# A list schedule that gives a token gather a longer way to its landing, and one conditional part at the end instead of two

## The chip, the cores and the metric

The kernel runs on 1 core of one Trainium2 chip. The metric is the device time of one execution in microseconds, as the median of several runs. Engines are named as in the profile: PE is TensorE's matmul, PEld its weight load, DVE is VectorE, ACT ScalarE, POOL GpSimd, SP SyncE. A "q" behind an engine's name marks rows of its sequencer.

## The reference, cut to what matters

Three layers follow each other: chunked attention, a dense layer, and a layer of 8 experts of which each of 3072 tokens uses the one with the largest logit. The change lies in the third.

```python
def _moe2_ref(x, modality_id, w_gate, modality_bias, w1, w2):
    logits = x @ w_gate + modality_bias[modality_id]      # (3072, 8)
    e_idx = np.argmax(logits, axis=1)
    probs = softmax(logits)
    gate_w = probs[np.arange(N), e_idx]
    for e in range(E):
        mask = e_idx == e
        h = np.maximum(x[mask] @ w1[e], 0.0)              # 512 -> 1024
        out[mask] = gate_w[mask, None] * (h @ w2[e])      # 1024 -> 512
```

## The kernel before, in words

**Order of the work.** All work is cut into units, each of one engine, with a length in the plan, a time until others see the result (`extra`), the units that it comes after and the tiles that it touches. `Plan.order` (lines 89 to 156) puts them in order before the program is built: each unit gets a rank, the longest way from it to the end in planned lengths, extras and slacks between units (600 ns where nothing else is given, 120 ns under the name HOP). Then, step by step, the unit is taken whose start, less 0.003 of its rank, is smallest (lines 119 to 134). A start is the latest of the engine's planned idle time, the planned ends of what it comes after, and a free slot for its tiles. What comes out is one order of instructions for each engine; the planned times themselves are not on the chip, where each engine waits for semaphores alone. A unit that waits holds back all that stands behind it on its engine.

**Stages.** Attention goes through 32 sub-blocks, the dense layer through 8 blocks of 384 tokens (`dense`, line 543), each with 16 pairs of products h and y on PE, in three float32r passes. One h of 384 columns is 12 matmuls, one y of three groups of 128 tokens is 9; each is a unit of 1950 ns in the plan. `in_turn` (line 533) fixes their order on PE over all tiles: h, h, y, h, y and so on, so that the first h of a tile stands between the last two y of the tile before. After each block, `routing` (line 569) computes the logits, scales the rows by their gates, stores them in DRAM (`yd`), and enters the tokens in a table of each expert's tokens. The table's entries come out of a small product on PE (`place`, line 677, unit `tm`, tile `tp`) and are added on DVE (`enter`, unit `ta`).

**Experts.** A tile of tokens is up to 384 tokens of one expert (3 groups of 128) or a small one of up to 128. Two tiles, e0 and e1, belong to the expert that is largest after 7 of the 8 blocks and start while the last block is still computed. Then come the lists that `plan_list` (line 797) computes on DVE: `planb`, 15 places for large tiles b0 to b14, and `plans`, 8 places for small ones s0 to s7. Six large tiles and one small one are always computed (`N_BIG`, `N_SMALL`). What is over these counts is computed in two conditional parts at the end of the program (lines 1083 to 1092): each loads a count of tiles from the tile `ei` into a register of each engine, compares, and branches over its instructions if nothing is over. With this input neither part is entered.

**Tokens of a tile** (`tokens`, line 857). DVE computes the tile's indices (`ids`, units `id`, tile `gi`), after the first h of the tile before. For each of the 3 groups POOL issues an indirect DMA that gathers 128 rows from DRAM (`gather`, line 889, unit `ga`, 1040 ns in the plan, tile `xg`); PE transposes them (`turn`, line 894, unit `tx`, tile `xp`, 4 small matmuls in line 896); ACT casts them (`high`, tile `xh`, line 899), DVE subtracts for the low part (`low`, tile `xl`, line 903). The first h of the tile reads both. The gather's time until others see the result is `extra=DMA_LAG + 800`, which is 2700 ns (line 910). The units `tx` have a boost, so that PE takes them as soon as the plan has them ready.

**Weights.** SP loads the expert's weights some units ahead (`weights`, line 926), ACT and DVE split them into high and low parts. Tiles of tokens and of weights share 36 slots of the tag `w`.

The scatter of a tile's results is an indirect DMA of POOL, too (`put`, line 1054).

Of the kernel before, what the change touches and what calls it, by code (L numbers as in the profile page):

```python
# [12 lines left out]
I32 = mybir.dt.int32  # L13
# [26 lines left out]
HOP = 120.0  # L40
DMA_LAG = 1900.0
BOOST = 20000.0
TAIL_BOOST = 40000.0
# [18 lines left out]
class Plan:  # L62
    """Units of work, each of one engine, put in order by a list schedule.

    A unit has an estimated length (and time until others see its result), the units it comes after and the tiles it
    touches; a tile holds a slot of its tag from the first unit that touches it to the end of the last.
    """

# [96 lines left out]
def kernel(  # L165
# [50 lines left out]
    g0 = const.tile([P, E], F32, name="g0")  # L216
    ei = const.tile([P, 3 + MAX_ST + E], I32, name="ei")
    masks = const.tile([QB, 3, P], BF16, name="masks")
# [24 lines left out]
    def U_seq(name, ns, steps, after=(), tiles=(), **kw):  # L243
        """A chain of VectorE units, one for each operation of a generator; name.k is the k-th, name itself the last."""
        gen = []

        def step(last):
            if not gen:
                gen.append(steps())
            next(gen[0], None)  # L250
            if last:
                for _ in gen[0]:
                    pass

        for i, n in enumerate(ns):
            last = i == len(ns) - 1
            U(name if last else f"{name}/{i}", "DVE", n, lambda last=last: step(last), [f"{name}/{i - 1}"] if i else after, tiles, **kw)

# [1 line left out]
    def constants():  # L260
# [40 lines left out]

        # the routing bias of each token, by its modality
        T.new("mi", "w", [P, NTILE, 2], I32)
# [20 lines left out]

# [1 line left out]
    # two heads go through the array at once, with zeros between them (q and k come with head pairs' columns as rows); the  # L326
    # first blocks' scores, for which the other engines have no time, are float32 products, the later three float32r passes
    def attention(n):
# [37 lines left out]
        def parts_of(key, i):  # L366
            """Of q all; of k the i-th half, the second heads' rows, which go into the right columns."""
            x, to = T[f"qk{n}"], T[f"qs{n}" if key == "q" else kb]
            if key == "q":
                return [to[:, 0], to[:, 1]], x[:, :, 0:QB]  # L370
            r = slice(64 * i, 64 * i + 64)
            return [to[r, e, :, P * i:P * i + P] for e in range(2)], x[r, :, QB:]
# [17 lines left out]
        def minima(i):  # L390
            """Of the negated scores."""
            for h in (2 * i, 2 * i + 1):
                dve.tensor_tensor_reduce(  # L393
                    out=T[f"pt{n}"][:, h, :], in0=T[f"sc{n}.{i // 2}"][:, h % 4, :], in1=mask, scale=-scale, scalar=3.0e38,
                    op0=ALU.add, op1=ALU.min, accum_out=T[f"mn{n}"][:, h:h + 1])
# [59 lines left out]

# [1 line left out]
    def conversion(f):  # L457
# [57 lines left out]

# [1 line left out]
    def prod_h(hp, xh, xl, wh, wl, n):  # L517
# [15 lines left out]
    def in_turn(h, y):  # L533
        """Keeps the products of both layers in turn: h, h, y, h, y, ..."""
        if chain:
            T.units[h][3].append(chain[-1][0])
            T.units[chain[-1][1]][3].append(h)
        if len(chain) > 1:
            T.units[h][3].append(chain[-2][1])
            T.units[y][3].append(chain[-1][1])  # L540
        chain.append((h, y))
# [23 lines left out]

# [1 line left out]
    O_t = {}  # L567

    def routing(j):
# [115 lines left out]
        def order(t, e):  # L685
            """Two experts' columns at a time."""
            return [f"lm{j}.{TPB - 1}.{e - 2}"] if e >= 2 else []
# [28 lines left out]

# [1 line left out]
    jobs = {}  # L718
# [37 lines left out]
    def plan_counts():  # L756
# [24 lines left out]
        yield  # L781
        # group of the s-th tile of the list = s + f[its expert]; f is summed up from its steps
        pool.memset(fb[:, E:E + 1], float(NG))
# [13 lines left out]
    def plan_list(nm):  # L797
        end, f, n, at, move = plan[nm]
        s16 = [P, n, E]
        c2, df, ex = parts(T["plan" + nm], n * E, E, n)  # L800
        dve.tensor_tensor(out=df, in0=f[:, 1:E + 1], in1=f[:, 0:E], op=ALU.subtract)
        yield
        c2 = c2.rearrange("p (s e) -> p s e", e=E)
        dve.tensor_tensor(out=c2, in0=bm(end, s16), in1=bc(iota[:, 0:n], s16), op=ALU.is_le)
        yield
        dve.tensor_reduce(out=ex, in_=c2, op=ALU.add, axis=AX.X)
        yield
        dve.tensor_scalar(out=ei[:, at:at + n], in0=ex, scalar1=float(E - 1), scalar2=None, op0=ALU.min)
        yield
        dve.tensor_tensor(out=c2, in0=c2, in1=bm(df, s16), op=ALU.mult)  # L810
        yield
        g = small([P, n], "g" + nm)
        dve.tensor_reduce(out=g, in_=c2, op=ALU.add, axis=AX.X)
        yield
        dve.tensor_scalar(out=g, in0=g, scalar1=f[:, 0:1], scalar2=None, op0=ALU.add)
        yield
        if move:
            dve.tensor_tensor(out=g, in0=g, in1=iota[:, 0:n], op=ALU.add)
            yield
        dve.tensor_scalar(out=g, in0=g, scalar1=float(NG), scalar2=None, op0=ALU.min)  # L820
        yield
        for i in range(n):
            jobs[nm, i].update(g=g[:, i:i + 1])
        last = 1 + MAX_ST + E + (0 if move else 1)
        dve.tensor_copy(out=ei[:, last:last + 1], in_=end[:, E - 1:E])
        yield

    def planning():
# [11 lines left out]
        U_seq("planb", [130] * 10, lambda: plan_list("b"), ["pc"], ["plan", "planb"])  # L840
        U_seq("plans", [100] * 9, lambda: plan_list("s"), ["pc"], ["plan", "plans"])
        ready = [f"st{NBLK - 2}.{t}" for t in seven]
# [14 lines left out]
    def tokens(s, prev):  # L857
        """Which tokens the tile has, their rows of y, and those turned for the products."""
        job, nm = jobs[s], nm_of(s)
# [48 lines left out]
        for t in range(nt):  # L908
            x = f"{nm}.{t}"
            U(f"ga{x}", "Pool", 1040, lambda t=t: gather(t), [f"id{nm}/{gi}"], [f"xg{x}", f"gi{nm}"], extra=DMA_LAG + 800, **F)  # L910
            U(f"tx{x}", "PE", 430, lambda t=t: turn(t), [f"ga{x}"], [f"xg{x}", f"xp{x}"], **F)
            U(f"tH{x}", "ACT", 480, lambda t=t: high(t), [f"tx{x}"], [f"xp{x}", f"xh{nm}"], **F)
            U(f"tL{x}", "DVE", 600, lambda t=t: low(t), [f"tH{x}"], [f"xp{x}", f"xh{nm}", f"xl{nm}"], **F)
# [12 lines left out]
    def weights(s, x, use, used, loads):  # L926
        """One tile of the expert's weights: loads, and the two parts; use is the product that it is for."""
        job = jobs[s]
# [65 lines left out]
    def small_step(s, g, used, y_after):  # L994
        """P tokens stay in the array and half of w1's columns pass by; their products are turned for the second layer."""
        nm = nm_of(s)
# [67 lines left out]

# [1 line left out]
    with tc.manual_schedule():  # L1066
# [15 lines left out]
        at = 1 + MAX_ST + E  # L1082
        for nm, n0, n1, col in (("b", N_BIG, MAX_ST, at), ("s", N_SMALL, E, at + 1)):
            cnt = nc.values_load(  # L1084
                ei[0:1, col:col + 1], min_val=0, max_val=n1,
                skip_runtime_bounds_check_because="a count of tiles that the number of tokens and experts bounds")
            with tc.If(cnt > n0):
                T.restart()
                chain.clear()
                begin.clear()  # L1090
                experts([(nm, i) for i in range(n0, n1)])
                T.emit()

# [29 lines left out]
def laid_out(name, inputs):  # L1123
    """q and k come in blocks, with two heads' columns as rows; v with a row's heads side by side, k and v with the memory rows after the context."""
    a = inputs[name]
# [50 lines left out]
```

## Time and profile before

| | |
|---|---|
| runs, us | 1023.49, 1021.09, 1030.64 (median 1023.49) |
| span of the profiled execution, us | 1021.5 |
| PE busy, us | 959.6 (94%) |
| DVE, ACT, POOL busy, us | 724.1, 479.0, 218.2 |
| mean granted TensorE clock | 0.975 |
| HBM read and written, MB | 97.20, 12.85 |

The profiled execution's own time is not recorded beside its span; of the three runs 1021.09 is 0.4 us under the span and 1023.49 is 2.0 us over it. The span goes from the first instruction to the last. The granted clock is a share of the full 2.4 GHz; its other level is 1.2 GHz.

How to read it: PE is busy nearly all of the span, so the questions are where it is not, and what it waited for there. A wait that the profile puts down to a DMA names the transfer whose landing came last.

### The profile page before, as it was taken

To read this page: it belongs to the slowest core of one execution; us is meant where nothing else is said; L and a number is where in the kernel's file an instruction comes from. 1 tells how busy PE (TensorE), PEld (TensorE's weight loads), DVE (VectorE), ACT (ScalarE), POOL (GpSimd) and SP (SyncE) were. 2 spreads that over 40 slices of the span, in tenths; PEclk is the share of its full clock that TensorE was granted. 3 is DMA by queue.
4 is the path that set the end of the run, shared out by engine and by line. 5 is a ranking of instruction groups with operands and counts; after the bars stand their busy time and mean duration, and the time that the engine had idled before them with its cause. 6 is when DMAs were issued, how large, how long until landed. Compare 5 with 4: busy or idle time off the path is not lost. (4 is left out here: it accounts for less than half of the span.)

```text
span 1021.5 us, 15964 instructions
## 1 busy us (share of the span) xinstructions
PE 959.6 (94%) x5356; PEld 847.6 (83%) x5356; DVE 724.1 (71%) x2031; ACT 479.0 (47%) x1273; POOL 218.2 (21%) x186
## 2 busy tenths in 40 slices
PE   6696899999999999999999999998999999999994
PEld 3575778889889889889889888997998888988983
DVE  5999988957966975984993993775975455544550
ACT  5666665626535544544553452224233344433541
POOL 6678552101201201111120210001012021112101
PEclk8789989999999999999999999999999999999998
DMA  9825421221231230221321211136057455456311
GB/s 285 271 77 169 132 70 50 89 90 50 78 101 30 82 117 20 81 89 42 99 72 59 88 43 42 42 101 218 22 179 232 153 169 176 138 163 208 129 49 44
DMA packets 99458, 110.99 MB, mean 109 GB/s; under 512 B 18623, under 2 KB 73695, under 8 KB 99360
## 3 DMA queue, kind: packets, MB, share of 16 engines
q1 hardware_dynamic: 95360, 96.96, 30.0%
q0 software_dynamic: 4000, 12.85, 3.8%
q8 instruction: 46, 0.75, 0.3%
q14 instruction: 52, 0.43, 0.1%
HBM read 97.20 MB, written 12.85 MB: 108 GB/s over the span
## 5 line engine op out<-in xcount | busy, mean ns | idle before, releaser
L411 POOL TENSOR_TENSOR pt<-pt,rs 96x512 f32<-96x512 f32 x64 | 83.8, 1328 | 411.7 <-DVE rs L406 332.3
L400 ACT ACTIVATE pt<-pt,mn 96x128 f32<-96x128 f32 x256 | 99.5, 392 | 42.6 <-DVE mn L393 42.5
L495 POOL TENSOR_TENSOR wm<-wm,wt 128x512 int32<-128x512 int32 x32 | 49.9, 1568 | 24.7 <-DVE wm L484 16.6
L400 ACT ACTIVATION_READ_ACCUMULATOR pt<-pt,mn 96x1 f32 x256 | 48.5, 190 | 0.0
L380 DVE TENSOR_TENSOR pad<-qk,pad 64x512 fp32r<-64x512 f32 x48 | 45.5, 947 | 0.7
L423 PE MATMUL pv<-px,v 128*64 128x96 f32 x512 | 30.9, 267 | 9.0 <-DVE mn L393 5.6
L423 PEld LDWEIGHTS pv<-px,v 128*64 128x64 f32 x512 | 24.5, 147 | 16.5 <-issue 12.7
L376 ACT CAST pad<-qk 64x512 fp32r<-64x512 f32 x48 | 29.5, 614 | 0.8 <-DMA qk<-in_k_dram 0.3
L502 POOL TENSOR_TENSOR wl<-wm,wh 128x512 fp32r<-128x512 f32 x16 | 24.8, 1548 | 5.2 <-ACT wh L498 5.2
L426 ACT CAST xh<-pv 128x384 fp32r<-128x384 f32 x32 | 15.1, 474 | 17.7 <-PE pv L423 17.7
L498 ACT CAST wh<-wm 128x512 fp32r<-128x512 f32 x32 | 19.6, 618 | 7.0 <-POOL wm L495 7.0
L393 DVE DVE_READ_ACCUMULATOR2_ANT mn<- 96x1 f32 x256 | 20.2, 79 | 0.0
L502 DVE TENSOR_TENSOR wl<-wm,wh 128x512 fp32r<-128x512 f32 x16 | 19.3, 1208 | 0.5 <-ACT wh L498 0.5
L480 DVE TENSOR_SCALAR wm<-wm 128x1024 int32<-128x1024 int32 x16 | 17.1, 1069 | 1.3 <-ACT wm L476 1.3
L890 POOL DMA_INDIRECT xge0.0_7148<-yd,gie x1 | 1.2, 1174 | 77.7 <-DMA rawxe0.1_7118<-in_moe_w_dram 77.7
L429 DVE TENSOR_TENSOR xl<-pv,xh 128x384 fp32r<-128x384 f32 x32 | 17.4, 547 | 0.0
L380 DVE TENSOR_TENSOR qs<-qk,qs 128x384 fp32r<-128x384 f32 x24 | 16.4, 682 | 0.5
L592 DVE DVE_READ_ACCUMULATOR2_ANT lg<- 128x1 f32 x192 | 15.7, 82 | 0.0
L376 ACT CAST qs<-qk 128x384 fp32r<-128x384 f32 x24 | 12.3, 512 | 0.2
L405 DVE TENSOR_SCALAR rs<-sm 96x8 f32<-96x8 f32 x32 | 9.6, 299 | 1.2 <-ACT pt L400 1.2
L632 DVE TENSOR_SCALAR ya<-ya,rg 128x512 f32<-128x512 f32 x16 | 7.4, 501 | 0.2
L406 DVE RECIPROCAL rs<-rs 96x8 f32<-96x8 f32 x32 | 6.4, 199 | 1.1
(6397 smaller groups left out, 3218.5 us busy)
## 6 DMA issues: line engine op xcount, KB each, us to landing
v<-in_v_dram SPq DMA_DIRECT2D x32, 256.0 KB, 2.7
qk<-in_k_dram SPq DMA_DIRECT2D x24, 256.0 KB, 3.2
qk<-in_q_dram SPq DMA_DIRECT2D x24, 192.0 KB, 3.3
yd<-ya SPq DMA_DIRECT2D x16, 256.0 KB, 2.1
pad<-in_k_dram SPq DMA_DIRECT2D x16, 128.0 KB, 3.9
yd<-yb SPq DMA_DIRECT2D x8, 256.0 KB, 2.5
qs<-in_q_dram SPq DMA_DIRECT2D x8, 192.0 KB, 4.5
wd0.0_114<-in_moe_w_in_dram SPq DMA_DIRECT2D x1, 512.0 KB
```

Of the source, the lines that this page charges most:

```text
L376: act.copy(out=to[0], in_=x)
L380: dve.tensor_tensor(out=to[1], in0=x, in1=to[0].bitcast(F32), op=ALU.subtract)
L393: dve.tensor_tensor_reduce(out=T[f"pt{n}"][:, h, :], in0=T[f"sc{n}.{i // 2}"][:, h % 4, :], in1=mask, scale=-scale, scalar=3.0e38, op0=ALU ...
L400: act.activation(out=pt[:, h, :], in_=pt[:, h, :], func=AF.Exp, bias=T[f"mn{n}"][:, h:h + 1], scale=-1.0, accum_out=T[f"sm{n}"][:, h:h + 1])
L411: pool.tensor_tensor(out=pt[:, half, :], in0=pt[:, half, :], in1=bc(T[f"rs{n}"][:, half], [QB, 4, P]), op=ALU.mult)
L423: pe.matmul(T[f"pv{n}"][r:r + 64, h // 2, :], T[f"v{n}"][:, D * h:D * h + D], T[f"px{n}"][:, h, :], start=True, stop=True)
L429: dve.tensor_tensor(out=T[f"xl{j}"][:, :, cols], in0=T[f"pv{n}"], in1=T[f"xh{j}"][:, :, cols].bitcast(F32), op=ALU.subtract)
L480: dve.tensor_scalar(out=mi, in0=mi, scalar1=3, scalar2=None, op0=ALU.logical_shift_left)
L495: pool.tensor_tensor(out=mi, in0=mi, in1=T[f"wt{f}"][:, i], op=ALU.add)
L498: (dve.tensor_copy if f in D_CH else act.copy)(out=T[f"wh{f}"][:, i], in_=T[f"wm{f}"][:, i])
L502: e.tensor_tensor(out=T[f"wl{f}"][:, i], in0=T[f"wm{f}"][:, i], in1=T[f"wh{f}"][:, i].bitcast(F32), op=ALU.subtract)
L592: dve.tensor_tensor_reduce(out=part(products), in0=part(y_at[t]), in1=T[f"wg{j}.{e // 2}"][:, e % 2], scale=1.0, scalar=0.0, op0=ALU.mult, ...
```

## The change

`GATHER_LAG = 6500.0` takes the place of `DMA_LAG + 800` (2700) as the planned time from a gather's issue unit to its landing. The scatter keeps `DMA_LAG + 800`. The two conditional parts become one, with the bodies of both. It is entered if a sum of two comparisons is above zero: `planb` writes "more than six large tiles" into the last column of the tile `plan`, and `plans`, which now comes after `planb`, adds "more than one small tile" and writes the sum into one column of `ei`, which is one column shorter. Comments and docstrings are left out of the changed file; line numbers stay but for the one added line.

```diff
 DMA_LAG = 1900.0
+GATHER_LAG = 6500.0
...
-    ei = const.tile([P, 3 + MAX_ST + E], I32, name="ei")
+    ei = const.tile([P, 2 + MAX_ST + E], I32, name="ei")
...
         for i in range(n):
             jobs[nm, i].update(g=g[:, i:i + 1])
-        last = 1 + MAX_ST + E + (0 if move else 1)
-        dve.tensor_copy(out=ei[:, last:last + 1], in_=end[:, E - 1:E])
+        if move:
+            dve.tensor_scalar(out=T["plan"][:, DM - 1:DM], in0=end[:, E - 1:E], scalar1=float(N_BIG), scalar2=None, op0=ALU.is_gt)
+        else:
+            dve.scalar_tensor_tensor(out=ei[:, at + n:at + n + 1], in0=end[:, E - 1:E], scalar=float(N_SMALL), in1=T["plan"][:, DM - 1:DM], op0=ALU.is_gt, op1=ALU.add)
         yield
...
-        U_seq("plans", [100] * 9, lambda: plan_list("s"), ["pc"], ["plan", "plans"])
+        U_seq("plans", [100] * 9, lambda: plan_list("s"), ["pc", "planb"], ["plan", "plans"])
...
-            U(f"ga{x}", "Pool", 1040, lambda t=t: gather(t), [f"id{nm}/{gi}"], [f"xg{x}", f"gi{nm}"], extra=DMA_LAG + 800, **F)
+            U(f"ga{x}", "Pool", 1040, lambda t=t: gather(t), [f"id{nm}/{gi}"], [f"xg{x}", f"gi{nm}"], extra=GATHER_LAG, **F)
...
         at = 1 + MAX_ST + E
-        for nm, n0, n1, col in (("b", N_BIG, MAX_ST, at), ("s", N_SMALL, E, at + 1)):
-            cnt = nc.values_load(
-                ei[0:1, col:col + 1], min_val=0, max_val=n1,
-                skip_runtime_bounds_check_because="a count of tiles that the number of tokens and experts bounds")
-            with tc.If(cnt > n0):
-                T.restart()
-                chain.clear()
-                begin.clear()
-                experts([(nm, i) for i in range(n0, n1)])
-                T.emit()
+        more = nc.values_load(
+            ei[0:1, at:at + 1], min_val=0, max_val=2,
+            skip_runtime_bounds_check_because="a sum of two results of comparisons")
+        with tc.If(more > 0):
+            T.restart()
+            chain.clear()
+            begin.clear()
+            experts([("b", i) for i in range(N_BIG, MAX_ST)] + [("s", i) for i in range(N_SMALL, E)])
+            T.emit()
```

## Rows read from the trace of the kernel before

**Rows 1.** The page, part 1: busy time of the engines, share, instructions.

```profile
PE 959.6 (94%) x5356; PEld 847.6 (83%) x5356; DVE 724.1 (71%) x2031; ACT 479.0 (47%) x1273; POOL 218.2 (21%) x186
```

**Rows 2.** Waits of PE from 640 us on: us in total, times, longest us.

```profile
PE xpb5.2_9557 L896 <- DMA xgb5.2_9510<-yd,gib: 2.0, 1, 2.0
PE xpe0.1_7220 L896 <- DMA xge0.1_7156<-yd,gie: 1.6, 1, 1.6
PE xpe0.0_7212 L896 <- DMA xge0.0_7148<-yd,gie: 1.2, 1, 1.2
PE xpb3.2_8875 L896 <- DMA xgb3.2_8828<-yd,gib: 0.9, 1, 0.9
...
PE xpb1.2_8193 L896 <- DMA xgb1.2_8146<-yd,gib: 0.8, 1, 0.8
PE hpxb0.0_8040 L521 <- ACT xhb L899: 0.7, 1, 0.7
PE xpb2.2_8534 L896 <- DMA xgb2.2_8487<-yd,gib: 0.7, 1, 0.7
PE xpb4.2_9216 L896 <- DMA xgb4.2_9169<-yd,gib: 0.5, 1, 0.5
```

**Rows 3.** Line 1084, register loads: ns min/median/max, first and last start us.

```profile
L1084 POOLq TENSOR_LOAD <-ei x2: 308/407/506, 1008.5 to 1014.5; - x2
```

**Rows 4.** Line 1087, the conditional parts: ns min/median/max, first and last start us.

```profile
L1087 POOLq EVENT_SEMAPHORE  x8: 17/43/3405, 1009.6 to 1015.3; - x8
...
L1087 PEldq COMPARE_BRANCH  x2: 3884/4128/4372, 1004.0 to 1008.5; - x2
...
L1087 POOLq COMPARE_BRANCH  x2: 45/45/45, 1009.1 to 1014.9; - x2
...
L1087 POOLq INC_SWDGE_SEM  x2: 1157/1172/1188, 1013.3 to 1015.4; - x2
```

**Rows 5.** Line 1171, the program's end: ns min/median/max, first and last start us.

```profile
L1171 POOLq DRAIN  x3: 40/107/4148, 1016.6 to 1021.3; - x3
```

**Rows 6.** Timeline of PE at e1's transposes: start us, us, engine, line, operation.

```profile
718.57 0.60 PE L896 MATMUL xpe1.0_7439<-ident,xge1.0_7382 128*128 128x128 f32 x4
...
719.36 0.95 PE L521 MATMUL hpxe0.3_7450<-xhe,ehxe0.3_7205 128*128 128x384 f32 x4
```

**Rows 7.** Timeline of PE at b1's transposes.

```profile
791.12 0.60 PE L896 MATMUL xpb1.0_8182<-ident,xgb1.0_8102 128*128 128x128 f32 x4
...
793.32 0.94 PE L521 MATMUL hpxb0.3_8200<-xhb,ehxb0.3_7921 128*128 128x384 f32 x4
...
795.49 0.39 PE L527 MATMUL ypb0.0_8105<-ehxb0.2_7910,ghxb0.2_8161 128*128 128x512 f32 x1
```

**Rows 8.** Timeline of PE at b5's transposes.

```profile
933.36 0.60 PE L896 MATMUL xpb5.0_9546<-ident,xgb5.0_9466 128*128 128x128 f32 x4
...
936.79 1.53 PE L521 MATMUL hpxb4.3_9564<-xhb,ehxb4.3_9393 128*128 128x384 f32 x4
...
940.52 0.39 PE L527 MATMUL ypb4.0_9469<-ehxb4.2_9358,ghxb4.2_9525 128*128 128x512 f32 x1
```

**Rows 9.** Windows: us, busy of PE, PEld, DVE, ACT, POOL, PEclk, DMA share, GB/s.

```profile
937.00:941.00 4.00, 4.00 (x16) 3.92 (x15) 0.69 (x1) 0.87 (x2) 1.00 (x1) 0.59 1.07 375
```

**Rows 10.** Timeline of PE at e0's and b0's transposes and first products, with tp7.

```profile
699.39 0.60 PE L896 MATMUL xpe0.2_7247<-ident,xge0.2_7181 128*128 128x128 f32 x4
...
706.08 0.86 PE L521 MATMUL hpxe0.0_7302<-xhe,ehxe0.0_7145 128*128 128x384 f32 x4
...
763.95 0.25 PE L679 MATMUL tp7.0_7919<-ab7.0_7689 128*128 128x192 f32 x1
...
774.69 0.60 PE L896 MATMUL xpb0.0_8017<-ident,xgb0.0_7980 128*128 128x128 f32 x4
...
778.43 0.97 PE L521 MATMUL hpxb0.0_8040<-xhb,ehxb0.0_7867 128*128 128x384 f32 x4 [0.68 <-ACT xhb L899]
```

**Rows 11.** Timeline of ACT at b0's transposes.

```profile
775.33 0.59 ACT L899 CAST xhb<-xpb0.0_8017 128x512 fp32r<-128x512 f32 x1 [2.02 <-PE xpb0.0_8017 L896]
```

## The prediction

> **What bounds the kernel now.** I read the page's first part, then PE's waits from 640 us on, then the timeline around each wait, and last the sequencer rows of the end. Nearly the whole span is TensorE's: 959.6 of 1021.5 us [rows 1]. From 640 us on, when the routed experts come into play, the list of PE's waits is short, and all but one of its longest entries have one form: the transposes of gathered tokens (line 896) wait for the gather's DMA, and once a first product waits for the cast behind the transposes [rows 2]. So in this stage a microsecond of PE wait is a microsecond of the run, and weights, activations and the other engines end no wait there. After the last product comes a stretch without PE work, in which Pool's queue sets the end [rows 3 to 5].
>
> **What a wait costs.** Undisturbed, two groups of transposes take 719.36 - 718.57 = 0.79 us, 0.44 for the first and 0.35 for each further one [rows 6], so three take 1.14. At b1 they took from 791.12 to 793.32, 2.20 us [rows 7]: 1.06 lost, of which 0.8 is the wait listed and 0.27 the restart. With the same restart b2, b3 and b4 lost 0.7, 0.9 and 0.5 plus three times 0.27, which is 2.91. e0 had two waits, 1.6 and 1.2 [rows 2], and lost 3.34. At b5 the three took from 933.36 to 936.79, so 2.29 were lost, and the product group behind took 940.52 - 936.79 = 3.73 us [rows 8] where the one after b1's took 2.17 (793.32 to 795.49): 1.56 more. The granted clock was 0.59 in that stretch [rows 9], part of it at the lower of the two levels, 1.2 GHz, after PE had stood still for 2.0 us. I book those 1.56 with the wait before them. b0 lost 778.43 - 774.69 - 1.14 = 2.60 [rows 10].
>
> **Part 1: the lag.** No instruction is added or removed; the schedule gives each engine another order. GATHER_LAG replaces 2700 ns by 6500, so the plan holds transposes ready 3.8 us later. In the plan a PE unit is 1950 ns, so they move back past two units of products; on the chip a unit is 2.17 us at most, so PE reaches them some 4.2 us later, less what it no longer waits.
>
> b1 to b5: these tiles are gathered right after the tile before has begun, and PE has ten units of that tile left when the transposes come (hpxb0.3 follows at 793.32). The latest landing against its place was b5's, 936.40; the third transposes would then stand at 933.36 + 4.2 + 0.79 = 938.3, so 1.9 us to spare. All of it goes: 1.06 + 2.91 + 2.29 + 1.56 = 7.8 us. What is late next is the tile's first product, and that is eight units off after the move.
>
> e0: its third transposes stood at 699.39 and its first product at 706.08, with three units between [rows 10]. Two units later one unit (2.1 us) is left, in which 0.35 of transposes, a cast of 0.59 [rows 11] and a subtraction, which I take as 0.7, must fit: 1.64. It fits by half a microsecond, and the low part is read only by the second third of the products. I take 3.3; the bounds are 0 and 3.34.
>
> b0: here nothing else can stand between, since the order of products is fixed by the code (line 533: h, h, y, h, y) and the first product of b0 comes right after the transposes. What can help is an earlier gather. Its indices wait for the table of the last block, whose small products (line 679) stood at 763.95 [rows 10], long after their inputs. PE picks the ready unit with the longest way to go. By the code's own costs and slacks the way from tp7 to b0's first product is 11,915 planned ns with the old lag; from the y that follows tp7 it is 11,790, from the h ahead of tp7 13,860, and from the y ahead of that 16,410. This is why tp7 stands where it does; with 15,715 it passes one unit, not two. So gather and landing come 2.1 us earlier, transposes run in one go at 774.69, and then ScalarE's three casts of 0.59 set the pace: the first began at 775.33 [rows 11], three in a row end at 777.16, not 778.43. I take 1.2; bounds 0 (no earlier gather) and 2.60.
>
> What moves with it: tp7's additions on DVE go ahead of one or two weight subtractions, and transposes' casts move on ACT and DVE. Neither engine ends a PE wait here except in the b0 case. The gathers themselves keep their places behind the tile's indices in Pool's queue; on SP the plan may shift a weight load by a unit, since token tiles hold their slots 3.8 us longer in the plan. No PE wait in [rows 2] ends on a weight, so I count that as nothing; uncovered it would be a wait like those of the list, 0.5 to 2.0 us.
>
> Part 1 sums to 7.8 + 3.3 + 1.2 = 12.3 us, between 0 and 13.8.
>
> **Part 2: one conditional part.** The two copies of a count (line 825) become two comparisons of one column each, and plans now follows planb. That is DVE time beside PE's products of e1, and no entry of [rows 2] ends on a DVE operation; uncovered it would be a wait like the smallest of the list, 0.5 us. At the end each engine loses one register load, one branch and one set of waits. Only Pool's copy matters: it goes through the first part, waits for the last scatter's landing (3.4 us), raises a semaphore (1.19 us), then goes through the second from its load at 1014.5 to the drain at 1016.6 [rows 3 to 5]. This second pass, 2.1 us, goes. The drain of 4.15 us stays, I assume. The bounds: 0, if the drain waits for something with a time of its own, and 4.2, if it works off two raises of 2.1 us each and has one left. I take 2.1, as the drain's row is one instruction that begins where the pass ends.
>
> On Pool the branch takes 0.05 us; on PE the same branch took 3.9 to 4.4 [rows 4]. The merged body is longer, so Pool's branch could come to cost what PE's does. It would lie beside the landing wait of 3.4 us, so at most 4.4 - 3.4 = 1.0 us of the 2.1 would be given back. The Trainium skill (Runtime: NRT & Kernel Launch, section Instruction fetch mechanics) says that a taken branch to a target outside the instruction window waits for a fetch; by that rule the longer body speaks against this part, with PE's branches agreeing and Pool's not showing it.
>
> **Sum.** 12.3 + 2.1 = 14.4 us: a span of 1007.1 us for the profiled execution's 1021.5. The three runs lie between 1021.09 and 1030.64 with a median of 1023.49; the span is beside the lower two, so I take the difference from the median: 1009.0 us.
>
> **The rivals.** (1) The wait only changes its place at e0 and b0: the first product waits for the cast or subtraction instead. For it: [rows 2] has such a wait at hpxb0.0, 0.7 us, and e0's spare is 0.5 us. Against: e0's casts have PE work beside them. Then 7.8 + 2.1 = 9.9 us are won: 1013.6, inside one per cent. (2) The end gives nothing, by the drain's own time or Pool's branch together: 12.3 won, 1011.2. For it: the drain is longer than anything else there. Against: nothing in flight is seen behind the last scatter's landing. (3) The change doesn't do what it says: transposes come later, but the gathers land later too, because they and the weight loads share the DMA engines, or the plan moves gathers and transposes together. Then only the end is won: 1021.4. Against: a gather is issued as soon as its indices are there, which the lag doesn't touch. (4) Slower: the longer lag puts transposes so late that each tile's first product waits, as at b0, long enough for the clock to fall as at b5. The place is the first h of e0 to b5; seven such tiles at b5's 3.85 us are 27 us, against 13.8 + 2.1 lost now, so 11 us slower: 1034. It decides against the change from 2.3 us per tile on. For it: b5's rows show the price. Against: b1 to b5 have eight units to spare, and only e0 and b0 are close.
>
> **How the numbers follow.** Forecast 0.62, rival 1 0.20, rival 2 0.08, rival 3 0.06, rival 4 0.04. A measurement of this kernel tells about 1 per cent from no change (the three runs alone lie 0.9 per cent apart), so faster by over 1 per cent means under 1013.3 us. Of the forecast 0.60 and of rival 2 0.07 lie there: 0.67. Within 1 per cent are rivals 1 and 3 and 0.03 of the others: 0.29. Slower: 0.04. The range reaches down to all waits gone and a drain halved (18.0 won, 1005.5) and up to rival 1 with another term of 3 us missing (1016.5).
>
> **What would show it.** Right: PE's waits from 640 us on lose every entry on a gather's DMA, transposes of b1 to b5 stand two product units further on, tp7 stands one unit earlier, the clock stays at 1.00 around b5, and Pool has one register load and one raise before its drain. Wrong: a wait of a first product (hpxe0.0, hpxb0.0) on xh or xl above 1.5 us; waits on gathers of the old size in new places; a drain that grew by what the pass lost; new waits on weights.

## The result, and the profile after

The changed kernel takes 1007.39 us (median of four runs, 1006.8 to 1008.51) beside 1023.13 of the kernel before in the same runs: a ratio of 0.984, with a 95% interval from 0.9801 to 0.9878. The profiled execution has a span of 1006.7 us, 14.8 less than the one before; its own time is 1008.51. The prediction was 1009.0 and a span of 1007.1, so the sum came out. Two of its terms did not, and they cancel in part, so some of that closeness is luck. Two of the ten runs of one experiment below, the merge alone, were slow (1342.14 and 1562.1 us, at a granted clock of 0.652 and 0.555) and are left out of its median.

First PE's waits, the same view and nearly the same stretch as [rows 2] (us in total, times, longest):

```profile
PE hpxb0.0_8040 L522 <- ACT xhb L902: 0.7, 1, 0.7
PE xpb0.2_8030 L899 <- DMA xgb0.2_7987<-yd,gib: 0.6, 1, 0.6
PE htxs0.1_10148 L1034 <- ACT hrxs0.1_10141 L1044: 0.2, 1, 0.2
```

That is the whole list from 630 us on (line numbers are up to three higher than before). The waits on gathers of e0 and of b1 to b5 in [rows 2] are gone; one at b0 is left, and b0's wait for the cast is unchanged. Before, b0 had two waits on gathers, one of 0.3 us and this one, which [rows 2] leaves out:

```profile
PE xpb0.1_8022 L896 <- DMA xgb0.1_7987<-yd,gib: 0.9, 1, 0.9
```

At b5 the transposes used to stand in one block and wait [rows 8]. Now, in the timeline of PE:

```profile
927.58 0.60 PE L899 MATMUL xpb5.0_9560<-ident,xgb5.0_9465 128*128 128x128 f32 x4
927.93 0.48 PE L528 MATMUL ypb4.0_9469<-ehxb4.2_9358,ghxb4.2_9528 128*128 128x512 f32 x1
...
930.09 0.60 PE L899 MATMUL xpb5.1_9590<-ident,xgb5.1_9485 128*128 128x128 f32 x4
930.53 0.60 PE L899 MATMUL xpb5.2_9595<-ident,xgb5.2_9495 128*128 128x128 f32 x4
930.88 0.94 PE L522 MATMUL hpxb4.4_9601<-xhb,ehxb4.4_9432 128*128 128x384 f32 x4
```

The first group stands one unit later (behind an h) and the other two groups two units later (behind the y that follows). No row has a wait in brackets. The granted clock in that stretch, transposes and the products behind them, columns as in [rows 9]:

```profile
927.00:935.00 8.00, 8.00 (x47) 7.21 (x46) 4.92 (x9) 4.60 (x9) 1.22 (x2) 1.00 0.42 160
```

1.00, the upper level, stands where 0.59 stood. PE was busy all 8 us ahead of and behind the transposes; the fall of the clock went with the wait.

At e0 the transposes stand two units later, as predicted. One unit, a y of block 7, is left between the third group and the first product:

```profile
697.09 0.60 PE L899 MATMUL xpe0.0_7247<-ident,xge0.0_7150 128*128 128x128 f32 x4
...
700.08 0.60 PE L899 MATMUL xpe0.2_7279<-ident,xge0.2_7182 128*128 128x128 f32 x4
702.60 0.86 PE L522 MATMUL hpxe0.0_7302<-xhe,ehxe0.0_7132 128*128 128x384 f32 x4
```

At b0 the small products tp7.1 and tp7.2 moved up by one unit, ahead of an h (tp7.0 moved further, to 743.92), and two short waits are left (in brackets: idle time, and what ended it):

```profile
758.60 0.25 PE L680 MATMUL tp7.1_7898<-ab7.1_7708 128*128 128x192 f32 x1
...
771.47 0.60 PE L899 MATMUL xpb0.0_8017<-ident,xgb0.0_7966 128*128 128x128 f32 x4
...
773.15 0.66 PE L899 MATMUL xpb0.2_8030<-ident,xgb0.2_7987 128*128 128x128 f32 x4 [0.65 <-DMA xgb0.2_7987<-yd,gib]
774.49 0.97 PE L522 MATMUL hpxb0.0_8040<-xhb,ehxb0.0_7870 128*128 128x384 f32 x4 [0.68 <-ACT xhb L902]
```

The end, to be read beside [rows 3 to 5] (ns minimum/median/maximum, first and last start):

```profile
L1086 POOLq TENSOR_LOAD <-ei x1: 498/498/498, 996.9 to 996.9; - x1
```

```profile
L1089 POOLq EVENT_SEMAPHORE  x4: 17/42/2323, 997.9 to 998.2; - x4
...
L1089 PEldq COMPARE_BRANCH  x1: 3778/3778/3778, 992.5 to 992.5; - x1
...
L1089 POOLq COMPARE_BRANCH  x1: 45/45/45, 997.5 to 997.5; - x1
...
L1089 POOLq INC_SWDGE_SEM  x1: 1188/1188/1188, 1000.5 to 1000.5; - x1
```

```profile
L1173 POOLq DRAIN  x3: 40/107/4148, 1001.8 to 1006.5; - x3
```

One load, one branch, one raise of a semaphore (INC_SWDGE_SEM); the drain has the same 4148 ns; Pool's branch costs 0.045 us as before. But there is one difference that the prediction did not have: the wait for the last scatter's landing is 2.32 us, where it was 3.41.

Where the time went, by stages. The starts of first products are read from the timelines of PE, and the stages are their differences in us:

| stage | before | after | won |
|---|---|---|---|
| start to block 7's first h | 633.93 | 634.10 | -0.17 |
| to e0's first h | 72.15 | 68.50 | 3.65 |
| to e1's first h | 34.74 | 34.94 | -0.20 |
| to b0's first h | 37.62 | 36.95 | 0.67 |
| to b5's first h (b1 to b5's transposes) | 180.74 | 173.06 | 7.68 |
| to PE's last product | 48.51 | 48.60 | -0.09 |
| to the span's end | 13.87 | 10.58 | 3.29 |
| span | 1021.55 | 1006.73 | 14.82 |

### The profile page after: what moved, and what is told of

Same layout as the page of the kernel before. It is cut to its first block, busy times and chain, and to the rows that moved or that the text cites. A ratio compares the mean times of both kernels' runs of the same rounds, so it can differ in the third digit from the quotient of the medians.

```text
span 1006.7 us, 15940 instructions
## 1 busy us (share of the span) xinstructions
PE 958.3 (95%) x5356; PEld 848.1 (84%) x5356; DVE 721.9 (72%) x2031; ACT 477.8 (47%) x1273; POOL 221.7 (22%) x186
## 5 line engine op out<-in xcount | busy, mean ns | idle before, releaser
L496 POOL TENSOR_TENSOR wm<-wm,wt 128x512 int32<-128x512 int32 x32 | 49.9, 1568 | 25.2 <-DVE wm L485 16.4
L893 POOL DMA_INDIRECT xge0.0_7150<-yd,gie x1 | 1.2, 1171 | 77.2 <-DMA rawxe0.1_7102<-in_moe_w_dram 77.2
```

The source lines that it names most:

```text
L496: pool.tensor_tensor(out=mi, in0=mi, in1=T[f"wt{f}"][:, i], op=ALU.add)
```

## The experiments

In what follows "the end" is the time from PE's last product to the span's end, and "from block 7" is the sum of the last six stages of the table (387.62 before, 372.63 after). That sum leaves out the first 634 us, which differ by up to 4.1 us between executions of kernels that are nearly alike there (632.5 to 636.6). It is therefore finer than the medians, but it is read from one execution of each kernel.

**Each part alone.** The lag on the kernel before:

```diff
-            U(f"ga{x}", ..., extra=DMA_LAG + 800, **F)
+            U(f"ga{x}", ..., extra=GATHER_LAG, **F)
```

> The lag alone, with both conditional parts kept as before. Theory (a wait of PE costs its length and a restart of 0.27 us; the second pass at the end costs 2.1 us): PE waits as in the changed kernel, Pool's second pass is back, 1007.4 + 2.1 = 1009.5 us. Rival (all 3.2 us by which the stretch behind the last product is shorter come from the merged part): 1010.6 us, with a last scatter that lands in 4.5 us as before. Rival (the end gives nothing): 1007.4 us.

Measured: 1011.27 us (1010.55 to 1012.49), ratio 0.988 [0.9864, 0.9897]; from block 7 374.97 us; PE's waits are b0's 0.8 and s0's 0.3 alone. The end is 13.85 us, as before. The lag is thus worth 12.7 us of the 15.0 in this view. In this execution b0's transposes waited for no gather, and e1's to b0's first product took 36.19 us, 0.8 less than in the changed kernel. The end speaks for the first rival, that the merge gives all of the 3.2 us there; 2.1 us for it was too little.

The merge alone, which is the changed kernel with the old lag:

```diff
-GATHER_LAG = 6500.0
+GATHER_LAG = 2700.0
```

> The merged part alone, with the old lag of 2700. Theory: all waits on gathers as before, one pass less at the end, 1023.1 - 2.1 = 1021.0 us; if b5's wait is again 2 us, the clock falls behind it again and costs 1.5 us. Rival (the end gives 3.2 us): 1019.9 us. Rival (the fall of the clock at b5 was an accident of one execution): no fall with the same wait.

Measured: 1020.1 us (median of eight runs, 1015.1 to 1023.82), ratio 0.997 [0.9947, 0.9993]; from block 7 383.53; the end is 10.27 us. So the merge gives 3.6 us at the end with the old lag (13.87 less 10.27) and 3.3 with the longer one (13.85 less 10.58), and again 2.1 was too little. PE's waits are those of [rows 2] with other sizes. The windows of this run show the clock again (columns as in [rows 9]; behind e0's waits, behind b0's, behind b5's):

```profile
697.00:700.50 3.50, 3.50 (x15) 3.41 (x14) 0.72 (x2) 0.60 (x2) 0.00 (x0) 0.53 1.05 378
778.50:782.50 4.00, 3.40 (x11) 3.40 (x12) 1.18 (x3) 0.54 (x1) 0.00 (x0) 0.57 0.40 132
935.50:939.50 4.00, 2.81 (x18) 2.80 (x19) 1.82 (x3) 1.05 (x3) 0.16 (x1) 1.00 1.07 383
```

The clock went to the lower level, 1.2 GHz, for most of a stretch at e0 (behind a wait of 2.2 us) and at b0 (behind 1.0, 0.3 and 0.7), and not at b5 (1.4), where it fell in the kernel before. A fall comes behind such waits, but not in a fixed place. The sizes of the waits are those of one execution.

**The size of the lag**, by the same line:

```diff
-GATHER_LAG = 6500.0
+GATHER_LAG = 4600.0
```

> The changed kernel with half the added lag, 4600. The order on PE shows the transposes of b1 to b5 one unit later than before, those of e0 one unit later, and two of three tp7 products where they stood before. Theory (each wait is set against the place of the transposes): waits of b1 to b4 (0.5 to 0.9) gone, b5's 2.0 down to 0.1 or less and no fall of the clock, e0 keeps one wait of 1.0, b0 loses 2.6 as before; 2.5 us over the changed kernel, 1009.9 us. Rival (the gain is from the order at large, not from these places): as the changed kernel, 1007.4 us, or half of the gain gone, 1014 us.

Measured: 1012.03 us, ratio 0.9883 [0.9866, 0.9899]; but from block 7 373.22, only 0.6 over the changed kernel, and PE waits at b0 (0.7 and 0.5) and s0 alone. The expected wait at e0 is not there. The profiled spans lie 3.1 us apart, and 2.5 of these lie in the first 634 to 636.6 us, ahead of all gathers; the changed kernel itself took 634.10 and 636.39 us for them in its two profiles. What is left of the 4.6 us between the medians no profile shows.

And with `GATHER_LAG = 10300.0`:

> The changed kernel with twice the added lag, 10300. The order on PE shows all three transposes of e0 right ahead of its first product, and tp7 two units earlier than in the changed kernel. Theory: nothing more to win at b1 to b5; e0's first product now waits for casts, about 1.3 us lost; b0's gather lands before PE comes to it, so its wait on the DMA (0.65) goes and only the wait for casts stays; 0.7 us over the changed kernel, 1008.1 us. Rival (a longer lag makes each tile's first product wait): over 1015 us.

Measured: 1008.8 us, ratio 0.9855 [0.9839, 0.9872]; from block 7 372.55. Here the transposes of e0 stand right before its first product, and rival 1 of the prediction shows itself at e0 (timeline of PE):

```profile
701.97 0.60 PE L899 MATMUL xpe0.2_7289<-ident,xge0.2_7184 128*128 128x128 f32 x4
703.35 0.96 PE L522 MATMUL hpxe0.0_7302<-xhe,ehxe0.0_7131 128*128 128x384 f32 x4 [0.78 <-ACT xhe L902]
```

It costs 1.2 us at e0 (69.71 against 68.50 us to e0's first h). Most of that is paid back at b0 (36.07 against 36.95), where the gathers come earlier and no wait for a DMA is left. So from 4600 to 10300 the place of the transposes is worth less than 1 us: what counts is that they stand behind the landing at all.

**The end.** Why does one part less give 3.3 to 3.6 us when its pass on Pool lasted 2.1? To tell a second part's own price from what comes with its length, a second part with a tiny body was put behind the merged one:

```diff
+        second = nc.values_load(
+            ei[0:1, at:at + 1], min_val=0, max_val=2,
+            skip_runtime_bounds_check_because="a sum of two results of comparisons")
+        with tc.If(second > 0):
+            nc.vector.tensor_copy(out=ei[:, at:at + 1], in_=ei[:, 0:1])
```

> The changed kernel with a second conditional part behind the one it has: the same flag is loaded again, and its body is a single small DVE copy. What is read is the end: from PE's last product to the span's end it took 13.9 us with two long parts, 10.2 to 10.6 with one; the last scatter took 4.5 to 4.6 us from issue to landing with two, 3.0 to 3.4 with one. Theory: a second part costs Pool a pass of 2.1 us whatever its length, while the scatter's later landing comes from instruction fetches of the second branches that share DMA engines with it, and a branch over a tiny body needs none: tail 12.3 to 12.7 us, scatter 3.0 to 3.4 us, as many instruction packets beside the scatter as in the changed kernel (4). Rival A: a second part delays the scatter by its loads and waits, however short: tail 13.6 to 13.9, scatter 4.5. Rival B: the pass of a tiny part hides in the landing wait: tail 10.2 to 10.6.

Measured: the end is 10.74 us (1009.21 us in all, ratio 0.9864 [0.9829, 0.99]); the scatter takes 3.0 us. So the theory was right on the scatter and wrong on the pass. The tiny part costs Pool a load of 0.30 us and a branch of 0.045, some 0.5 us in all, with no raise:

```profile
L1095 POOLq TENSOR_LOAD <-ei x1: 304/304/304, 999.4 to 999.4; - x1
```

A raise of 1.2 us therefore belongs to the long body, which has DMAs of Pool in it, and not to a conditional part as such; it is over half of the 2.1 us. Whether the DMAs or the length bring it was not tested. What delays the scatter can be seen in the DMA queues. Packets, MB and share of the 16 engines' time during the last scatter, from its issue to the end of its landing wait, first before (4.6 us):

```profile
q0 software_dynamic: 80, 0.20, 14.6%
q14 instruction: 4, 0.03, 2.8%
q8 instruction: 1, 0.02, 2.8%
```

after (3.4 us):

```profile
q0 software_dynamic: 80, 0.20, 16.1%
q14 instruction: 3, 0.02, 2.8%
q8 instruction: 1, 0.02, 1.8%
```

the lag alone, with two parts (4.7 us):

```profile
q0 software_dynamic: 80, 0.20, 17.3%
q8 instruction: 2, 0.03, 4.5%
q14 instruction: 4, 0.03, 2.7%
...
out_dram<-bys0.0_10185,sxs POOLq DMA_INDIRECT x1, 4.6
```

and the merged part with the tiny one behind (3.2 us):

```profile
q0 software_dynamic: 80, 0.20, 16.2%
q14 instruction: 3, 0.02, 3.0%
...
out_dram<-bys0.0_10185,sxs POOLq DMA_INDIRECT x1, 3.0
```

The scatter is always the same 80 packets. Beside them the two kernels with two long parts have one instruction packet more on q14, and their large ones on q8 take 2.8% of 16 times 4.6, which is 2.06 us, and 4.5% of 16 times 4.7, which is 3.4 us for two; after the change the one packet takes 1.8% of 16 times 3.4, 0.98 us. They are read here as what branches fetch: PE's second branch begins at 1008.5 and takes about 4 us [rows 4], so it lies beside the scatter, issued at 1008.74. The Trainium skill (Runtime: NRT & Kernel Launch, section Instruction fetch mechanics) says that an engine fetches its instructions by DMA in blocks of 16 KiB, and that a taken branch out of the window forces such a fetch. The packets of q8 agree (44 for 0.72 MB on the page after, 16.4 KB each), and so do PE's branches, 3.3 us over the long body and 0.24 over the tiny one in the run with both; Pool's branch of 0.045 us, over a body of the same kind, shows no wait for one. Other runs fall in line: without any instruction packet beside it the last scatter landed in 2.6 us (the run without a part, below), without one of q8 in 3.0 to 3.2 (six runs with one long part), beside one short one of q8 in 3.4 (both profiles of the changed kernel), and beside the long ones in 4.6. That the fetches delay the scatter is how these views are read here. No run delayed the scatter by fetches alone.

To see what the remaining part costs, it was left out; large tiles over six and small ones over one are then not computed, and with this input there are none:

```diff
-        more = nc.values_load(
...
-        with tc.If(more > 0):
...
```

> The changed kernel without any conditional part (large tiles over six and small ones over one are then never computed; with this input there are none). Theory: Pool's remaining pass, raise included, goes as the second one went, and the scatter has no branch's instruction fetch beside it: tail 10.4 less 2.1, so 8.0 to 8.5 us, with the drain of 4.15 us still there, and a scatter of 3.0 us or less from issue to landing. Rival A: the raise of 1.2 us belongs to the drain and stays: tail 9.2 to 9.6. Rival B: the drain waits for something with a time of its own: tail unchanged, 10.2 to 10.6, with a longer drain.

Measured: the end is 6.84 us, under every one of the three expectations (1005.02 us in all, ratio 0.9816 [0.9779, 0.9852]). The rows of Pool's last scatter and of its drain:

```profile
997.12 0.98 POOL L1058 DMA_INDIRECT out_dram<-bys0.0_10185,sxs  x1 [3.32 <-ACT bys0.0_10185 L1055]
```

```profile
L1164 POOLq DRAIN  x3: 40/107/5373, 996.9 to 1002.8; - x3
```

The drain begins beside the scatter's issue (its row starts at 996.9 and lasts 5.37) and ends 4.2 us after that issue (996.9 + 5.37 - 998.10), while the scatter lands 2.6 us after its start. So the drain has a time of its own of about 4.15 us behind Pool's last work, and runs beside the landing; a scatter that lands later than that was not tested. What waits for the landing is the skipped part: 2.3 us, and then its raise of 1.2. That is 3.5 of the 3.7 us by which this end is shorter than the changed kernel's 10.58.

If so, that price should go when the part is passed before the last scatter is there. The last scatter was moved behind it (its source tile takes the room of bias and masks):

```diff
             T.emit()
+        late[0]()
```

> The changed kernel with the last scatter (small tile s0) issued behind the conditional part instead of ahead of it; its source tile takes the room of the bias and the masks, which are done with by then. Without any conditional part the end took 6.84 us from PE's last product, and the drain ran beside the scatter's landing; with one part Pool waits 2.0 to 2.3 us for that landing, then 1.19 us for the raise, and drains behind both. Theory: only these two are the part's price, so when Pool has them ahead of the last scatter, beside the landing of b5's last scatter (issued 3.3 us before PE's end, 3.0 to 3.4 us on its way, then 1.2 us and half a us to the next instruction, so 0.8 us late for the last scatter), the end takes 7.2 to 8.0 us and the time falls by some 2.8 us. Rival A: the scatter behind the part waits for more than Pool (all engines, their branches' fetches): 9 us or more. Rival B: the landing wait and the raise follow the last scatter wherever it stands: 10.2 to 10.6 as in the changed kernel.

Measured: 1005.26 us, ratio 0.9818 [0.9803, 0.9833]; the end is 8.56 us, 2.0 less than the changed kernel's and 0.6 more than the theory's upper bound.

```profile
L1098 POOLq INC_SWDGE_SEM  x1: 1168/1168/1168, 997.2 to 997.2; - x1
```

```profile
999.55 0.98 POOL L1059 DMA_INDIRECT out_dram<-bl,ei  x1 [4.64 <-issue]
```

```profile
L1183 POOLq DRAIN  x3: 40/113/5726, 999.3 to 1005.6; - x3
```

The wait for the last scatter is gone. But Pool's queue still stands from 995.0 to the raise at 997.2, with no row for it. That is 3.3 us behind the issue of the scatter before, at 993.93, so it is most likely the wait for that one's landing, which the theory had reckoned in. PE's branch ends then too, at 997.0, and no run parts the two.

```profile
L1098 POOLq EVENT_SEMAPHORE  x4: 17/43/43, 994.8 to 995.0; - x4
```

```profile
993.93 0.98 POOL L1067 DMA_INDIRECT out_dram<-byb5.2_10129,sxb  x1 [2.52 <-DMA out_dram<-byb5.1_10125,sxb]
```

Two terms were too small: from the raise's end at 998.4 to the scatter it takes 1.15 us and not 0.5, and the drain ends 4.5 us behind the scatter's issue (999.3 + 5.73 - 1000.53) and not 4.2. The mechanism held.

**b0.** The changed kernel gained 0.7 us there where 1.2 was predicted. With the old lag for b0's gathers alone:

```diff
-            U(f"ga{x}", ..., extra=GATHER_LAG, **F)
+            U(f"ga{x}", ..., extra=DMA_LAG + 800 if nm == "b0" else GATHER_LAG, **F)
```

> The changed kernel with the old 2700 ns for b0's three gathers alone, so that tp7 and b0's gathers stand where they stood before. Theory: b0's transposes wait for the gathers as before, and from the first of them to b0's first product it takes 3.7 us again, where the changed kernel has 3.0: 0.7 us more than the changed kernel's 1007.4, 1008.1. Rival A: the step of the prediction was right in size and something else ate 0.5 us: 1.2 more, 1008.6. Rival B: b0's own lag does nothing and the 0.7 is from elsewhere: 1007.4.

Measured: 1008.54 us (ratio 0.9859 [0.9831, 0.9886]); from block 7 373.19, with 37.90 from e1's to b0's first product, 0.95 over the changed kernel's 36.95, and the two waits on gathers back (1.1 and 0.3). So the lag is what won this, and between the theory's 0.7 and rival A's 1.2 the run does not decide. Why it won less than predicted is seen in the landings, as the DMA view lists them (the last number: us from issue to landing). The old lag:

```profile
xgb0.0_7980<-yd,gib POOLq DMA_INDIRECT x1, 3.5
xgb0.1_7987<-yd,gib POOLq DMA_INDIRECT x1, 5.7
xgb0.2_8002<-yd,gib POOLq DMA_INDIRECT x1, 5.4
```

The longer lag (the run with the tiny second part, whose b0 is that of the changed kernel):

```profile
xgb0.0_7966<-yd,gib POOLq DMA_INDIRECT x1, 7.0
xgb0.1_7971<-yd,gib POOLq DMA_INDIRECT x1, 5.8
xgb0.2_7987<-yd,gib POOLq DMA_INDIRECT x1, 5.9
```

The gathers left earlier and took longer. But they don't always: the same gathers in the run with the lag alone landed in time, and PE waited for none of them.

```profile
xgb0.1_7971<-yd,gib POOLq DMA_INDIRECT x1, 4.7
xgb0.2_7987<-yd,gib POOLq DMA_INDIRECT x1, 5.2
```

In the run without a part they did as well (5.1 and 5.3 us, no wait listed). In these two b0's stage took 36.19 and 36.24 us, 1.4 less than before. So the lag won between 0.7 and 1.4 us at b0, by the execution, and the prediction's 1.2 lies within. Would still earlier gathers help? With 7500 ns for b0, and a boost of 3500 for the last block's table products:

```diff
-            U(f"tm{j}.{t}", ..., hop=HOP if j == NBLK - 1 else PE_SLACK)
+            U(f"tm{j}.{t}", ..., hop=HOP if j == NBLK - 1 else PE_SLACK, boost=3500.0 if j == NBLK - 1 else 0.0)
...
-            U(f"ga{x}", ..., extra=GATHER_LAG, **F)
+            U(f"ga{x}", ..., extra=7500.0 if nm == "b0" else GATHER_LAG, **F)
```

> The changed kernel with 7500 ns for b0's gathers and a boost of 3500 ns for the last block's small table products, so that these go two product units earlier than in the changed kernel and b0's transposes stand one to two units ahead of its first product. Theory: b0's gathers are late only because tp7 stands late; issued some 4 us earlier they land before their transposes, and both waits that the changed kernel has left there go (0.65 on the gather, 0.7 on the cast), with what the restart costs: 1.9 us won, 1005.5. Rival A: the landing is set by the DMA engines, which are 94 per cent busy there, and not by the issue: gathers land where they did, and the time stays 1007.4. Rival B: the earlier transposes wait longer at their new place, and later work on DVE (the weights' subtractions behind tp7's additions) is late: 1009 or more.

Measured: 1006.03 us, ratio 0.983 [0.9803, 0.9857]; PE's only wait from 630 us on is s0's 0.3; e1's to b0's first product takes 35.25 us, 1.7 less than in the changed kernel (theory 1.9) and 0.9 to 1.0 less than in the two runs just named. The landings of the second and third gather are longer still (7.0 and 6.8 us), and no longer matter:

```profile
xgb0.2_7931<-yd,gib POOLq DMA_INDIRECT x1, 6.8
```

**Both gains together**, beside the changed kernel on the same chip. The last scatter behind the part, with the earlier gathers of b0:

> The last scatter behind the conditional part together with the earlier gathers of b0 (7500 ns and the boost of the last block's table products). Theory: the two lie in different places and add up: no wait of PE at b0, an end of 7.2 to 8.0 us, some 4.5 us under the changed kernel, 1003. Rival: they don't add up, since the time of an execution wanders by as much at its start: 1004.5 to 1006.

The changed kernel itself:

> The changed kernel again, beside the two above on the same chip, as what they are to be compared with: 1007.0 to 1008.5, an end of 10.2 to 10.6 us, and PE's waits of 0.6 to 0.7 us at b0 only. If it comes out as fast as the two, their gains are not there.

Measured: 1004.98 us (1004.1 to 1005.69), ratio 0.982 [0.9807, 0.9834], against 1009.98 us (1006.63 to 1010.75), ratio 0.986 [0.9842, 0.9877]. The intervals do not overlap, if narrowly, and from block 7 it is 368.81 against 372.33 us: 3.5 us won, 1.7 at b0 and 1.8 at the end (8.69 against 10.51). So in this view they add up. The end of 8.69 is again over the theory's 8.0, for the two terms named above. Both medians are some 2 us above what was expected, and that of the two together lies in the rival's range; the changed kernel's start took 636.39 us here and 634.10 in its first profile.

## Why the prediction was right, and where it was not

- b1 to b5, predicted 7.8 us, the wait's restart and the clock included: 7.68. Each of the four pieces had its row, and the wait did not come back at the first products, eight units off. Booking the clock's 1.56 us with the wait before it holds: the changed kernel and every experiment but the merge alone show a clock of 1.00 from 634 us to 990 us, and the merge alone shows falls behind other waits on gathers. A wait doesn't always bring one: with the old lag for b0 alone the same waits at b0 (1.1, 0.3, 0.7) left the clock at 1.00. So the 1.56 was the price of that execution.
- e0, predicted 3.3 us: 3.65, of which some comes back as the 0.20 at e1. Two units were passed, one was left, no wait took their place. The last cast and subtraction did fit; with no unit left, at 10300, the cast did not, by 0.8 us. Rival 1 named the right mechanism, and only that one unit kept it out.
- b0, predicted 1.2 us: 0.67 in this execution. The order was right (tp7.1 and tp7.2 one unit earlier, transposes in the same place). The step that failed is "gather and landing come 2.1 us earlier, transposes run in one go". Counted from e1's first product, the third gather left 1.8 us earlier (766.90 less 737.54 after, 771.97 less 740.82 before), but it needed 6.2 us to the end of the wait for it, where it had needed 5.1, beside DMA engines with a share of 0.94 (after, 764 to 773 us). So of the three transposes one still waited 0.65 us. The landing was taken as a constant of the transfer; it is one of its moment, and in two other runs with the same order it came in time and the stage won 1.4 us. The three casts were reckoned a little too long: from 775.33 three of 0.59 end at 777.10 and not at 777.16, and where nothing held them up they took 1.56 us (771.48 to 773.04 in the lag alone).
- Part 2, predicted 2.1 us: 3.29, and 3.6 in the merge alone. "The drain of 4.15 us stays, I assume" was right: 4148 ns in all kernels that pass the part behind the last scatter. The pass of 2.1 us went. The term that was missing lies in the landing wait, which was taken as given (3.4 us): with one long part it is 2.0 to 2.3. The second branches' fetches are the likely reason, not a shown one. The bounds of 0 to 4.2 held it, for another reason than the one given for them.
- Pool's branch did not come to cost a fetch, though its body is longer; the reserve of 1.0 us against it was not needed.
- Rival 2 was right that the drain has a time of its own, and wrong on what follows. A drain that begins when Pool's queue comes to it moves with whatever stands ahead of it. Rivals 3 and 4 did not come: gathers of b1 to b5 are as early as before, and their transposes have units to spare.

The errors, 0.5 too much at b0 against 1.2 too little at the end and 0.35 at e0, with some tenths the other way, leave 0.4 us.

## What to carry to other kernels

In a hand-made schedule the planned time of a transfer has to be its landing under load, not its time alone: planned too short, every use stands in front of its data, and the compute engine pays the wait, a restart, and at times its clock. Planned too long it costs little as long as units are left in front of the first use. At a program's end look at what stands ahead of a long fixed instruction in its queue; a skipped conditional part with a long body waited there for Pool's DMAs in flight, and instruction packets, most likely those of its branches, shared the DMA engines with them.

## What was not expected of the hardware

- A skipped part with a long body that holds Pool's DMAs cost about 3.5 us with the last scatter ahead of it (landing wait and raise), a tiny one without them 0.5 us.
- Pool's drain of 4.15 us at the end ran beside a scatter's landing of 2.6 us, and ended 4.2 us behind the scatter's issue.
- An indirect gather of 256 KB took 3.1 to 8.2 us from issue to landing, by its moment (200 of them in eight runs, median 4.3). The Trainium skill (DMA: Bandwidth & Descriptors, section Anatomy of one DMA) gives a fit for a transfer from Pool of 2.0 us plus its bytes over 436,000 per us: as an estimate 2.6 us for these 262,144 bytes. The shortest here is 0.5 us above that and the longest three times as long, so no run bears the fit out under this load; the measurement decides.
